# Banded attention with a gated MLP: K without one copy of the global keys, score blocks of 192, 224, 224 and 192 keys, and another order of weights in the values

## Chip, core and metric

The kernel runs on one NeuronCore of a Trainium2 chip. The metric is the device time of one execution in microseconds (us), the median of several runs. The engines are PE (TensorE, matrix products), DVE (VectorE), ACT (ScalarE) and POOL (GpSimd); SP issues the DMAs.

## What is computed

Eight batches with eight heads of 64 columns; 512 local tokens and 32 global ones. A global token attends to all 544 tokens. A local token attends to the 32 global tokens and to the local ones at a distance of at most 32. The result, token by token with all heads side by side, goes through a gated MLP: a product of two projections, then two more matrices.

```python
k_all = np.concatenate([k_g, k_l], axis=2)
v_all = np.concatenate([v_g, v_l], axis=2)
out_g = np.matmul(sm(scale * np.matmul(q_g, k_all.transpose(0, 1, 3, 2))), v_all)
mask = np.abs(pos[:, None] - pos[None, :]) <= window          # window = 32
s_ll = np.where(mask, scale * np.matmul(q_l, k_l.transpose(0, 1, 3, 2)), -1000000000.0)
s_lg = scale * np.matmul(q_l, k_g.transpose(0, 1, 3, 2))
out_l = np.matmul(sm(np.concatenate([s_lg, s_ll], axis=-1)), np.concatenate([v_g, v_l], axis=2))
...
h = (x @ w1) * (x @ w2) @ w3
return (h @ w_out).astype(np.float32)
```

## The kernel before

**Keys and scores.** A head's 512 local queries are four blocks of 128. A block needs its own 128 keys, 32 keys on either side (one side only at the ends) and the 32 global keys. The host lays K out so that each block's keys lie in one piece: k0, g, k1, g, k2, g, k3 (k0 to k3 are the local blocks, g the global keys), 608 columns. WIN (L22) gives each block's first column and width: (0, 192), (96, 256), (256, 256), (416, 192). The middle blocks read 256 columns, in which the global keys stand twice; the mask hides the second copy. `load_k2` (L372) fetches K of two heads, the 64 rows of either head one above the other in 128 partitions; `scores` (L479) makes all blocks of both heads, one head on the upper and one on the lower 64 rows of the array. Only the first two heads go through `scores1` (L466), one at a time. Each float32 product is executed as two instructions.

**Softmax.** `minus_max` (L494, DVE) reads a block's scores from PSUM, adds the mask from the constants `cs`, writes the block to the tile P and its minimum to `small`. `exps` (L503, ACT) takes exponentials in place and sums them. PAT (L23) says where each block lies in P.

**Turning the weights.** The values need the exponentials with the keys in the partitions. For the first eight heads PE transposes them (`transposes`), and ACT and DVE copy the pieces into the tiles PT (local keys) and G (global keys; `pieces`, `weights_hi`). From the ninth head on DVE transposes blocks of 32x32 (`turn` for the edges and the global columns, `turn_own` for the block's own keys); the latter go through DRAM (tile od) and come back turned as the tile own. There every number is split into a high and a low float32r part, both in PT and G.

**Values.** `values` (L615) makes the product with V for one head in two halves x. A half begins with a product with the global keys' V (L630), then come two key blocks j (L636). From the ninth head on each key block has two products: y = 0 is the high part of the weights with 128 columns of V (high and low part of V), y = 1 is the low part with V's 64 high columns. So V, the stationary operand, has 128, 64, 128, 64 columns in a row.

**MLP.** `first` (L787 to L789) and `second` (L819 to L821) run for 256 tokens at a time between the heads; at the start `fold` (L921) multiplies the last two matrices into one.

**Order.** PLAN (L70) lists all steps by number, with the engine that runs each; the list is the program's order, and every engine works its own steps through in that order. The numbers are those of the calls of `add`. All DMAs go out from SP in this order.

Of the kernel before, what the change touches and what calls it, by code (L numbers as in the profile page):

```python
# [20 lines left out]
KD = 608  # L21
WIN = [(0, 192), (96, 256), (256, 256), (416, 192)]  # L22
PAT = [0, 192, 448, 704]  # L23
PW = 896
# [6 lines left out]
def i(ap):  # L31
# [8 lines left out]
    qgl=(250, 461), vgh=606, vgl=(620, 1290), mmax=(437, 502), exps=(545, 592), inv=350, mul=(420, 740),  # L40
    hi=(587, 231, 231, 475, 294, 203, 256), hi_dve=(683, 260, 260, 540, 0, 0, 292), lo=(692, 253, 253, 559, 540, 247, 280), half=(470, 530), sum=520, join=485,
# [4 lines left out]
    scores1=1650, scores2=1910, ownt=780, ownl=(691, 1300), values32=(1180, 1130), gscores32=930, take=(446, 521), shiftp=(330, 300, 420),  # L46
# [24 lines left out]
    1V 790S 386S 3V 328S 791S 0S 390S 329S 8S 12S 16S 389S 5V 387P 792P 152S 846S 388D 793D 391P 795D 794A 797D 796A  # L71
    392D 798A 9D 393A 799D 10A 394D 800A 11D 395P 14A 13D 801P 20S 396A 397A 15D 802D 24S 18A 813P 845S 803D 804D 17D
    19D 805A 808A 806A 248P 807V 814D 816D 28S 809P 815A 399S 817A 158S 818D 820D 811P 819A 821A 22A 21D 825P 830A 23D
    826D 249P 32S 164S 827A 829A 828A 847P 822D 832A 810D 26A 823S 25D 27D 36S 900S 831V 812D 30A 258P 868D 848D 850D
    833P 835P 849A 852D 854D 853A 851A 29D 31D 398S 250P 863A 855A 862V 870D 40S 872D 400P 403S 874D 34A 33D 856P 834A
    875A 251P 166A 873A 836D 35D 44S 857A 259P 260P 837D 859D 869A 858D 7V 401D 899S 261P 861A 38A 860D 37D 864P 866P
    39D 871A 48S 876D 877S 42A 165D 167D 41D 865A 879P 43D 886A 885A 404P 52S 880D 884A 881A 330S 883A 262P 405D 882A
    46A 2V 887P 45D 406A 47D 252P 888A 56S 407D 824S 901P 953S 50A 49D 253P 902D 51D 867A 889P 54A 53D 60S 331A 55D
    903A 159D 254P 922D 924D 58A 64S 57D 255P 256A 59D 263P 264P 265P 890A 68S 257D 268P 269P 923A 891V 402S 154A 839V
    904D 906D 892V 270P 908D 408P 160A 842V 266A 267D 333A 62A 61D 878S 909A 925A 271P 63D 272P 332D 72S 65D 66A 843A  # L80
    67D 409A 273P 926D 76S 410A 928D 70A 278P 69D 71D 929A 274P 907A 844D 80S 917A 275P 153D 412S 893V 279P 276D 277D
    954S 280P 74A 73D 281P 905A 75D 84S 927A 282P 896D 78A 910P 77D 930D 931S 283P 284P 912D 911A 79D 933P 915A 914A
    155D 88S 82A 916V 81D 913A 285P 83D 92S 894A 413A 334D 918P 895D 286A 335S 414D 840A 920P 287D 841V 86A 932S 937A
    85D 87D 288P 289P 936A 838V 938A 934D 96S 290P 90A 89D 935A 291P 91D 919A 161D 955P 100S 94A 93D 336A 939A 95D 104S
    292P 921A 337V 940A 423S 976D 293P 956D 957A 978D 958D 941P 98A 960D 961A 294P 97D 99D 959A 415P 962D 110S 102A
    980D 295P 963A 943P 101D 982D 416A 103D 105D 106A 107D 964P 411S 942A 296A 965D 116S 298P 108V 944A 299P 968A 109D
    300P 301P 970A 424A 417D 945V 122S 112A 1008S 977A 111D 113D 983A 967D 946V 302P 303P 304P 297D 114A 115D 969A 966A
    971A 950D 305P 118A 128S 425D 1007S 979A 117D 951A 119D 981A 972P 974P 124A 984D 123D 985S 120A 125D 306A 121D 987P
    992A 426P 308P 309P 310P 947V 126A 993V 307D 134S 427A 990D 127D 130A 129D 991A 311P 140S 131D 312P 897A 428D 898V
    132A 313P 429A 133D 989D 988A 146S 430D 1082S 973A 952V 431D 975A 136A 314P 135D 432S 315P 316A 994A 137D 1155S  # L90
    948A 1009P 338S 141D 142A 949V 138V 139V 1040D 439S 1010D 1041A 1012D 1081S 1230S 1011A 1014D 318P 319P 986S 1013A
    1016D 148A 1042D 320P 1017A 1015A 321P 322P 433S 147D 149D 150A 143D 1043A 1024D 1028A 323P 324P 325P 151V 144A
    1044D 1046D 1025D 1026S 995P 997P 326A 317D 1029V 1032S 1047A 327D 418S 1045A 996D 145V 168A 1048D 1049S 1083P 156A
    6V 169D 182S 998A 157D 4V 162A 440A 999D 1001D 170S 3087P 3089P 1002A 163D 176S 1004D 1030A 1003D 3088P 3090P 1027S
    1031A 441D 1020A 1005A 1000V 419A 421A 3091P 1058D 1021V 420V 3095A 1057D 1114D 3093P 184A 422D 1229S 1061A 183D
    185D 1033S 172A 3092P 3094P 3101P 3102P 186A 171D 173D 178A 1059S 177D 1022A 187D 174A 179D 450S 1018A 175D 180A
    1084D 1085A 1086D 200S 1088D 1087A 188S 1116D 1115A 3096D 1089A 1062V 1065S 1019V 1023V 434S 1006V 3097A 1118D
# [187 lines left out]
def band_attention_glu_kernel(  # L285
# [20 lines left out]
    nc = tc.nc  # L306
# [6 lines left out]
    S = 544  # L313
# [13 lines left out]
    mask = cs[:, 128:384]  # L327
    masks = [cs[:, 384:576], mask, mask, mask[:, 0:192]]
# [13 lines left out]
    def constants():  # L342
        nc.sync.dma_start(cs, cst)

# [183 lines left out]
    def transposes(n):  # L528
        P = Ps[n % NP_]
        tt = T["tt", n] = ps_1.tile([128, 2, 4, 128], F32, tag="pu", name=f"t{n}", bufs=2)  # L530
        for e in range(4):
            nc.tensor.transpose(tt[:, 0, e, :], P[:, 256 * e : 256 * e + 128], ident)
        for e in range(3):
            nc.tensor.transpose(tt[:, 1, e, :], P[:, 256 * e + 128 : 256 * e + 256], ident)
# [50 lines left out]
    def pieces(n, e):  # L585
        plain = n < NF
        PT, G = M["PT", plain], M["G", plain]
        if e in (4, 5):
            TGr, TGg = T["TG", n // 4]
            c = 32 * (n % 4)  # L590
            if e == 4:
                r = TGr[:, n % 4].rearrange("p (a b q) -> p a b q", a=2, b=2)
                return r, gslots(PT, 0), gslots(PT, 1)
            return TGg[:, c : c + 32], G[0:32, 0:32], G[32:64, 0:32]
        if not plain:
            return T["own", n].rearrange("p (a x) -> p a x", a=4), *(PT[:, 2:6, y].rearrange("p a j q -> p a (j q)") for y in range(2))
        tt = T["tt", n]
        if e == 0:
# [16 lines left out]
    def values(n, x):  # L615
# [16 lines left out]
        for j, o, s0, s1 in ((2, 0, 0, 7), (3, 160, 1, 7)) if x else ((0, 0, 1, 7), (1, 128, 1, 8)):  # L632
            v = (T["vr", n // 2][:, j] if plain else T["vs", n // 2][:, n % 2, j]).rearrange("p a b -> p (a b)")
            for y in range(1 if plain else 2):
                r = 64 if y else 128
                nc.tensor.matmul(av[0:r, o : o + 32 * (s1 - s0)], v[:, 0:r], PT[:, s0:s1, y, j], start=False,  # L636
                                 stop=(j % 2 == 1 and (plain or y == 1)), skip_group_check=True)
# [395 lines left out]
    def head(n):  # L1033
# [354 lines left out]

    for key, users in late:
        after[key] += [u for u in users if u != key]  # L1390
# [73 lines left out]
```

## Time and profile before

| | |
|---|---|
| median of 3 runs | 809.75 us (809.15 to 809.78) |
| profiled execution | 809.29 us, of which its span 807.5 us |
| busy: PE, DVE, ACT, POOL | 794.4, 531.2, 455.3, 390.9 us |
| granted PE clock, mean | 0.995 |
| DMA | 128.85 MB in 191554 packets |

The span reaches from the first to the last instruction; the rest of the execution's time lies around it. Busy time is summed over stages that differ: the start (to 21 us), the first eight heads with the folding of matrices (to 105), the passage to the split numbers (to 150), the long stretch with heads and MLP together (to 702) and the MLP's rest. A chain of waits is followed back from the last instruction: each piece is what released the piece behind it.

### The profile page before, as it was taken

What the parts mean: (1) busy time and instruction counts of PE and PEld (TensorE: products, weight loads), DVE (VectorE), ACT (ScalarE), POOL (GpSimd) and SP (SyncE); (2) the same over time, 40 slices, a digit from 0 to 9 for tenths busy, and PEclk for the clock granted to TensorE, in tenths of its full rate; (3) what the DMA queues carried; (4) which work ended last, traced back from release to release, by engine and by line L of the source; (5) the groups of instructions that cost most, each with busy time, mean ns of one, the idle gap of its engine ahead of it and who ended that gap; (6) DMA issues with size and microseconds to landing.
All of it is one profiled execution on the core that took longest, in us unless ns stands there. A gap on an engine that the chain in (4) does not pass through costs nothing.

```text
span 807.5 us, 17227 instructions
## 1 busy us (share of the span) xinstructions
PE 794.4 (98%) x5608; PEld 704.6 (87%) x5608; DVE 531.2 (66%) x1504; ACT 455.3 (56%) x1290; POOL 390.9 (48%) x603
## 2 busy tenths in 40 slices
PE   9999989799999999999999999999999999999998
PEld 7656568699999999999999999999998999999997
DVE  4877978878777666677688867666576587612111
ACT  4767877776555545466665757665566554412011
POOL 1122354666555657656546556546556565412110
PEclk9999999999999999999999999999999999999999
DMA  8887877866557457565666656666664555300000
GB/s 275 266 267 226 262 193 193 207 171 187 160 151 206 122 155 180 144 188 138 162 174 170 202 157 169 177 171 173 187 171 130 137 152 153 97 27 14 15 27 26
DMA packets 191554, 128.85 MB, mean 160 GB/s; under 512 B 114472, under 2 KB 151592, under 8 KB 191464
## 3 DMA queue, kind: packets, MB, share of 16 engines
q1 hardware_dynamic: 191464, 127.75, 57.7%
q8 instruction: 44, 0.72, 0.4%
q14 instruction: 46, 0.38, 0.1%
HBM read 92.73 MB, written 34.96 MB: 158 GB/s over the span
## 4 chain that ended last, share of the span: by engine, by line
PE 94%; DVE 2%; ACT 1%; DMA 1%; SPq 1%; issue 0%; POOL 0%; ACTq 0%; DVEq 0%; POOLq 0%
PE bp L787 8%; PE ap L787 8%; PE acc L821 8%; PE acc L820 8%; PE acc L819 8%; PE bp L788 7%; PE bp L789 7%; PE ap L788 7%; PE ap L789 7%; PE w L921 7%; PE av L636 7%; PE s L491 6%; PE av L630 2%; PE sg L686 2%; DMA own<-od 1%; PE idle L364 1%
## 5 line engine op out<-in xcount | busy, mean ns | idle before, releaser
L787 PE MATMUL bp<-x,w12h 128*128 128x256 f32 x544 | 153.0, 281 | 0.0
L787 PE MATMUL ap<-x,w12h 128*128 128x256 f32 x544 | 152.5, 280 | 0.0
L788 PE MATMUL bp<-x,w12h 128*128 128x256 f32 x544 | 151.0, 278 | 0.0
L789 PE MATMUL bp<-x,w12l 128*128 128x256 f32 x544 | 150.8, 277 | 0.0
L788 PE MATMUL ap<-x,w12h 128*128 128x256 f32 x544 | 150.6, 277 | 0.0
L789 PE MATMUL ap<-x,w12l 128*128 128x256 f32 x544 | 150.5, 277 | 0.0
L504 ACT ACTIVATE P<-P,small 128x256 f32<-128x256 f32 (+1 forms) x256 | 121.6, 476 | 25.9 <-DVE small L500 25.1
L787 PEld LDWEIGHTS ap<-x,w12h 128*128 128x128 f32 x544 | 102.1, 188 | 4.0 <-issue 2.9
L787 PEld LDWEIGHTS bp<-x,w12h 128*128 128x128 f32 x544 | 102.6, 189 | 3.3 <-issue 2.2
L788 PEld LDWEIGHTS bp<-x,w12h 128*128 128x128 f32 x544 | 102.7, 189 | 0.7
L788 PEld LDWEIGHTS ap<-x,w12h 128*128 128x128 f32 x544 | 102.3, 188 | 0.7
L789 PEld LDWEIGHTS bp<-x,w12l 128*128 128x128 f32 x544 | 102.6, 189 | 0.0
L789 PEld LDWEIGHTS ap<-x,w12l 128*128 128x128 f32 x544 | 102.2, 188 | 0.0
L500 DVE CUSTOM_DVE_ANT_0 P<-s,cs 128x192 f32<-128x192 f32 (+1 forms) x256 | 86.1, 383 | 7.1 <-PE s L491 4.2
L650 DVE TENSOR_TENSOR u<-av,cb 64x352 f32<-64x352 f32 x112 | 55.7, 517 | 33.3 <-ACT cb L417 30.9
L417 ACT COPY cb<-av 64x352 f32<-64x352 f32 x71 | 30.6, 446 | 61.3 <-PE av L636 46.8
L636 PE MATMUL av<-PT,vs 128*128 128x192 f32 x448 | 62.0, 266 | 0.6 <-POOL PT L420 0.6
L921 PE MATMUL w<-wo,w3f 128*128 128x512 f32 x128 | 58.7, 597 | 0.3 <-DVE wo L845 0.3
L491 PEld LDWEIGHTS s<-kq,qp 64*128 64x128 f32 x496 | 43.3, 186 | 15.6 <-issue 6.5
L420 POOL TENSOR_TENSOR TT<-TT 128x352 fp32r<-128x352 f32 x38 | 38.5, 1013 | 35.7 <-ACT TT L417 20.5
L491 PE MATMUL s<-kq,qp 64*128 64x192 f32 (+1 forms) x496 | 55.4, 362 | 0.0
L636 PEld LDWEIGHTS av<-PT,vs 128*128 128x128 f32 x448 | 53.0, 164 | 2.7 <-POOL PT L420 0.8
(818 smaller groups left out, 1872.5 us busy)
## 6 DMA issues: line engine op xcount, KB each, us to landing
od<-tw SPq DMA_DIRECT2D x56, 256.0 KB, 2.6
own<-od SPq DMA_DIRECT2D x224, 64.0 KB, 2.4
raw_w<-in_w_t_dram SPq DMA_DIRECT2D x24, 512.0 KB, 4.9
kq<-in_kd_t_dram SPq DMA_DIRECT2D x32, 304.0 KB, 3.6
kpr<-in_kp_t_dram SPq DMA_DIRECT2D x32, 272.0 KB, 3.9
out_dram<-o_None SPq DMA_DIRECT2D x33, 256.0 KB, 2.8
qp<-in_q_t_dram SPq DMA_DIRECT2D x32, 256.0 KB, 3.7
R<-rd SPq DMA_DIRECT2D x64, 128.0 KB, 3.1
```

What stands on the lines that cost most here:

```text
L491: nc.tensor.matmul(st[:, x, c : c + w], q[r, 128 * e : 128 * e + 128], k[r, o : o + w], start=(e % 2 == 0), stop=True, skip_group_check=True)
L500: nc.vector.tensor_tensor_reduce(blk(n, e), s, masks[e], -0.125, 3.0e38, ALU.add, ALU.min, T["mn", n][:, e : e + 1])
L504: nc.scalar.activation(blk(n, e), blk(n, e), AF.Exp, bias=T["mn", n][:, e : e + 1], scale=-1.0, accum_out=T["sm", n // 2][:, n % 2, e : e ...
L636: nc.tensor.matmul(av[0:r, o : o + 32 * (s1 - s0)], v[:, 0:r], PT[:, s0:s1, y, j], start=False, stop=(j % 2 == 1 and (plain or y == 1)), s ...
L650: nc.vector.tensor_add(T["u", n // 2][r : r + 64, x], T.pop(("av", n, x))[r : r + 64, 0:352], T["cb", n][r : r + 64, x])
L787: nc.tensor.matmul(d, wh[:, k, c, :], x[:, 0, 0:w], start=(k == m % 2 == 0), stop=False, skip_group_check=True)
L788: nc.tensor.matmul(d, wh[:, k, c, :], x[:, 1, 0:w], start=False, stop=False, skip_group_check=True)
L789: nc.tensor.matmul(d, wl[:, k, c, :], x[:, 0, 0:w], start=False, stop=(k == 3), skip_group_check=True)
L819: nc.tensor.matmul(a, gh[:, m % 2, sl], wh[:, c], start=(m == 0), stop=False, **part)
L820: nc.tensor.matmul(a, gh[:, m % 2, sl], wl[:, c], start=False, stop=False, **part)
L821: nc.tensor.matmul(a, gl[:, m % 2, sl], wh[:, c], start=False, stop=(m in (5, 7)), **part)
L921: nc.tensor.matmul(T["w34", t], T["w3f", t, j // 4][:, j % 4], T["wo"][:, j], start=(j == 0), stop=(j == 7))
```

## The change

The layout in DRAM stays. `load_k2` fetches each row in two pieces, k0, g, k1 and k2, g, k3, and leaves out the copy of g between them: 576 columns. The blocks become 192, 224, 224 and 192 columns wide. The order inside the third block differs now from that inside the second (own keys before the global ones), so each of them has a mask of its own. The new step `order_masks` makes them from the loaded constants with two small copies on POOL; it stands early in PLAN as 3877V (V is POOL), between 0S, the load of the constants, and 5V, the clearing of G. Where P is read, the places follow. In the second key block of each half of the values, the product with 64 weight columns goes ahead of that with 128. Otherwise PLAN is the same. `COST` is not read by this list order.

```diff
-KD = 608
-WIN = [(0, 192), (96, 256), (256, 256), (416, 192)]
-PAT = [0, 192, 448, 704]
-PW = 896
+KD = 576
+WIN = [(0, 192), (96, 224), (256, 224), (384, 192)]
+PAT = [0, 192, 416, 640]
+PW = 832
...
-    mask = cs[:, 128:384]
-    masks = [cs[:, 384:576], mask, mask, mask[:, 0:192]]
+    masks = [cs[:, 384:576], cs[:, 128:352], cs[:, 352:576], cs[:, 128:320]]
...
+    def order_masks():
+
+        nc.gpsimd.tensor_copy(cs[:, 320:352], cs[:, 352:384])
+        nc.gpsimd.tensor_copy(cs[:, 352:384], cs[:, 128:160])
...
-        nc.sync.dma_start(kr, kd_t[b, 2 * p : 2 * p + 2].rearrange("h d s -> (h d) s"))
+
+        k = kd_t[b, 2 * p : 2 * p + 2].rearrange("h d s -> (h d) s")
+        nc.sync.dma_start(kr.rearrange("p (a s) -> p a s", a=2), view(k, 0, [320, 2], [1, 288]))
...
-        nc.vector.transpose(view(t, 32, [256, 3], [64, 3], [1, 32]), view(P, 160, [32, 3], [256, 3], [1, 32]))
-        nc.vector.transpose(t[:, 7, 1], P[:, 128:160])
+        nc.vector.transpose(view(t, 32, [256, 2], [64, 3], [1, 32]), view(P, 160, [32, 2], [224, 3], [1, 32]))
+        nc.vector.transpose(view(t, 480, [64, 2], [128, 2], [1, 32]), view(P, 128, [96, 2], [448, 2], [1, 32]))
...
-        nc.vector.transpose(view(t[:], 0, [32, 4], [128, 4], [1, 32]), view(P, 0, [256, 4], [32, 4], [1, 32]))
+        nc.vector.transpose(view(t[:], 0, [64, 2], [32, 2], [128, 4], [1, 32]), view(P, 0, [448, 2], [256, 2], [32, 4], [1, 32]))
...
-            3: (tt[96:128, 1, 0:3].rearrange("p a b -> p (a b)"), G[0:32, 160:S], None),
-            6: (tt[0:32, 1, 0], G[0:32, 32:160], None),
+            3: (tt[96:128, 1, 0:3:2], g_own[:, :, 1], None),
+            6: (tt[0:32, 1, 0:3:2], g_own[:, :, 0], None),
...
-            for y in range(1 if plain else 2):
+            ys = (0,) if plain else (1, 0) if j % 2 else (0, 1)
+            for y in ys:
                 r = 64 if y else 128
...
-                [("s", n) if n < 2 else ("sp", n // 2), *([("mmax", n, e - 1)] if e else [("load", "cs")])], minus_max, n, e)
+                [("s", n) if n < 2 else ("sp", n // 2), *([("mmax", n, e - 1)] if e else [("masks",)])], minus_max, n, e)
...
+    add(("masks",), only("POOL", 200, True), -30.0, [("load", "cs")], order_masks)
```

What stands in a row on PE for one pair of heads' scores (s from kq, the K of the pair, and qp, its Q), with the neighbours, before and then now. The last numbers of a row are the partitions or weight columns and the columns of the product:

```order
L921 MATMUL w_0_225<-wo,w3f_0_181 128x512
L491 MATMUL s_0_271<-kq_215,qp_152 128x192 x2
L491 MATMUL s_0_271<-kq_215,qp_152 128x256 x2
L491 MATMUL s_1_276<-kq_215,qp_152 128x256 x2
L491 MATMUL s_1_276<-kq_215,qp_152 128x192 x2
L921 MATMUL w_1_298<-wo,w3f_0_220 128x512
```

```order
L929 MATMUL w_0_227<-wo,w3f_0_183 128x512
L497 MATMUL s_0_273<-kq_217,qp_154 128x192 x2
L497 MATMUL s_0_273<-kq_217,qp_154 128x224 x2
L497 MATMUL s_1_278<-kq_217,qp_154 128x224 x2
L497 MATMUL s_1_278<-kq_217,qp_154 128x192 x2
L929 MATMUL w_1_300<-wo,w3f_0_222 128x512
```

The rows stay where they were; the four in the middle (two rows, two heads each) have 224 columns in place of 256.

On PE the values of one head (av from G, PT, and the global keys' V vgs and the pair's V vs), both halves, up to the first product of the MLP behind them, before and now:

```order
L630 MATMUL av_2444<-G_1039,vgs 128x288
L636 MATMUL av_2444<-PT_1046,vs_2274 128x192
L636 MATMUL av_2444<-PT_1046,vs_2274 64x192
L636 MATMUL av_2444<-PT_1046,vs_2274 128x224
L636 MATMUL av_2444<-PT_1046,vs_2274 64x224
L630 MATMUL av_2444<-G_1039,vgs 128x256
L636 MATMUL av_2444<-PT_1046,vs_2274 128x224
L636 MATMUL av_2444<-PT_1046,vs_2274 64x224
L636 MATMUL av_2444<-PT_1046,vs_2274 128x192
L636 MATMUL av_2444<-PT_1046,vs_2274 64x192
L787 MATMUL bp_0_0_2457<-x_0_0_1814,w12h_88 128x256
```

```order
L637 MATMUL av_2446<-G_1041,vgs 128x288
L644 MATMUL av_2446<-PT_1048,vs_2276 128x192
L644 MATMUL av_2446<-PT_1048,vs_2276 64x192
L644 MATMUL av_2446<-PT_1048,vs_2276 64x224
L644 MATMUL av_2446<-PT_1048,vs_2276 128x224
L637 MATMUL av_2446<-G_1041,vgs 128x256
L644 MATMUL av_2446<-PT_1048,vs_2276 128x224
L644 MATMUL av_2446<-PT_1048,vs_2276 64x224
L644 MATMUL av_2446<-PT_1048,vs_2276 64x192
L644 MATMUL av_2446<-PT_1048,vs_2276 128x192
L795 MATMUL bp_0_0_2459<-x_0_0_1816,w12h_88 128x256
```

In both halves the fourth and the fifth product have changed places: the 128-wide one comes last.

On POOL, where the next head's weights are written into PT (TGr holds the turned weights of the global queries; CAST writes the high part, the TENSOR_TENSOR behind it the low part), with the semaphores that each instruction waits for, before and now:

```order
L420 TENSOR_TENSOR PT_1046<-TGr_1713,PT_1046 128x2x2x32 [waits Activation_49]
L526 TENSOR_TENSOR u_1585<-u_1585,R_1612 128x256 [waits DMAHW5_49,DMAHW4_49]
L417 CAST kph_1948<-kpr_1822 128x544 [waits DMAHW2_49,PE_49]
L417 CAST PT_1046<-TGr_1713 128x2x2x32 [waits PE_49,Pool_49]
L420 TENSOR_TENSOR PT_1046<-TGr_1713,PT_1046 128x2x2x32 [waits PE_49,Pool_49]
```

```order
L426 TENSOR_TENSOR PT_1048<-TGr_1715,PT_1048 128x2x2x32 [waits Activation_49]
L532 TENSOR_TENSOR u_1587<-u_1587,R_1614 128x256 [waits DMAHW5_49,DMAHW4_49]
L423 CAST kph_1950<-kpr_1824 128x544 [waits DMAHW2_49,PE_49]
L423 CAST PT_1048<-TGr_1715 128x2x2x32 [waits PE_49,Pool_49]
L426 TENSOR_TENSOR PT_1048<-TGr_1715,PT_1048 128x2x2x32 [waits Pool_49]
```

The instructions stand as before; the low part's writer no longer waits for PE, since the high part's writer ahead of it now waits for the later product.

## Rows read from the trace of the kernel before

**Rows 1.** The page's chain that ended last, share of the span by engine.

```profile
PE 94%; DVE 2%; ACT 1%; DMA 1%; SPq 1%; issue 0%; POOL 0%; ACTq 0%; DVEq 0%; POOLq 0%
```

**Rows 2.** Stretches: length, then PE, PEld, DVE, ACT, POOL busy, clock, DMA share, GB/s.

```profile
21.00:105.00 84.00, 83.93 (x325) 49.51 (x326) 69.20 (x191) 62.23 (x168) 20.55 (x31) 1.00 0.82 253
...
150.00:702.00 552.00, 551.77 (x4181) 510.49 (x4182) 397.36 (x1145) 329.64 (x959) 325.19 (x509) 1.00 0.62 165
```

**Rows 3.** Waits, whole run: us in total, times, longest; PE's two longest and POOL's.

```profile
PE av L630 <- DVE small L717: 3.8, 1, 3.8
PE av L630 <- ACT P L504: 2.8, 1, 2.8
...
POOL PT L417 <- PE av L636: 65.1, 24, 7.0
```

**Rows 4.** Scores: group of the page; PE's timeline (start, us) in short windows; chain.

```profile
L491 PE MATMUL s<-kq,qp 64*128 64x192 f32 (+1 forms) x496 | 55.4, 362 | 0.0
...
280.84 0.55 PE L491 MATMUL s<-kq,qp 64*128 64x192 f32 x4
...
281.00 0.60 PE L491 MATMUL s<-kq,qp 64*128 64x256 f32 x4
...
281.22 0.60 PE L491 MATMUL s<-kq,qp 64*128 64x256 f32 x4
...
280.64 1.72 PE s L491 x16
282.36 0.31 PE bp L787
```

**Rows 5.** The chain in order of time (start, us, what), first head's scores.

```profile
7.46 1.71 PE s L476 x8
```

**Rows 6.** Groups by shape on DVE, the masked minimum: busy us, mean ns | idle before.

```profile
L500 DVE CUSTOM_DVE_ANT_0 P<-s,cs 128x256 f32<-128x256 f32 x128 | 49.7, 416 | 0.2
L500 DVE CUSTOM_DVE_ANT_0 P<-s,cs 128x192 f32<-128x192 f32 x128 | 43.3, 350 | 6.8 <-PE s L491 4.2 <-PE s L476 1.4
```

**Rows 7.** Values: weight loads by shape (PEld), then the chain around one head's values.

```profile
L636 PEld LDWEIGHTS av<-PT,vs 128*128 128x128 f32 x224 | 42.6, 190 | 1.9
L636 PEld LDWEIGHTS av<-PT,vs 128*64 128x64 f32 x224 | 30.7, 137 | 0.8 <-POOL PT L420 0.8
...
294.66 0.23 PE acc L821
294.89 0.13 PE av L630
295.02 0.41 PE av L636 x4
295.43 0.12 PE av L630
295.55 0.39 PE av L636 x4
295.95 0.14 PE bp L787
...
296.44 0.11 PE bp L788
```

**Rows 8.** DMA issues of the page: count, KB each, median us from issue to landing.

```profile
od<-tw SPq DMA_DIRECT2D x56, 256.0 KB, 2.6
...
kq<-in_kd_t_dram SPq DMA_DIRECT2D x32, 304.0 KB, 3.6
```

**Rows 9.** The chain in order of time, its two longest pieces between 105 and 150 us.

```profile
112.78 5.26 DMA own<-od
...
143.41 4.66 DMA own<-od
```

**Rows 10.** DVE's timeline at the start: start, us, instruction, idle before and releaser.

```profile
7.03 0.72 DVE L705 CUSTOM_DVE_ANT_1 Pg<-sg,cs 64x544 f32<-64x544 f32 x1 [5.90 <-DMA cs<-in_cst_dram]
...
9.49 0.42 DVE L500 CUSTOM_DVE_ANT_0 P<-s,cs 128x256 f32<-128x256 f32 x1
```

More of the change, by code (lines that the diff above doesn't have):

```diff
@@ L39 @@
     kh=703, kl=(790, 1500), qh=617, ql=(620, 1290), vh=404, vl=(545, 746), kph=647, kpl=(726, 1374), qgh=298,
-    qgl=(250, 461), vgh=606, vgl=(620, 1290), mmax=(437, 502), exps=(545, 592), inv=350, mul=(420, 740),
-    hi=(587, 231, 231, 475, 294, 203, 256), hi_dve=(683, 260, 260, 540, 0, 0, 292), lo=(692, 253, 253, 559, 540, 247, 280), half=(470, 530), sum=520, join=485,
+    qgl=(250, 461), vgh=606, vgl=(620, 1290), mmax=(437, 470), exps=(545, 568), inv=350, mul=(420, 740),
+    hi=(587, 231, 231, 366, 294, 203, 366), hi_dve=(683, 260, 260, 416, 0, 0, 416), lo=(692, 253, 253, 559, 540, 247, 280), half=(470, 530), sum=520, join=485,
     joing=750, xh=405, xl=(411, 740), cg=610, mg=790, eg=840, ng=820, wg=(683, 292), ga=588, gb=691, gh=620,
@@ L45 @@
     gtrans=465, own=355, turn=650, gturn=1010, edge=(513, 520), edgel=(520, 960), first=1372, second=1382, fold=860,
-    scores1=1650, scores2=1910, ownt=780, ownl=(691, 1300), values32=(1180, 1130), gscores32=930, take=(446, 521), shiftp=(330, 300, 420),
+    scores1=1543, scores2=1610, ownt=780, ownl=(691, 1300), values32=(1180, 1130), gscores32=930, take=(446, 521), shiftp=(330, 300, 420),
 )
@@ L76 @@
[L76 to L80, printed above, removed]
@@ new lines @@
+    23D 826D 249P 32S 164S 827A 829A 828A 847P 822D 832A 810D 26A 823S 25D 27D 36S 900S 831V 812D 30A 258P 868D 848D
+    850D 833P 835P 849A 852D 854D 853A 851A 29D 31D 398S 250P 863A 855A 862V 870D 40S 872D 400P 403S 874D 34A 33D 856P
+    834A 875A 251P 166A 873A 836D 35D 44S 857A 259P 260P 837D 859D 869A 858D 7V 401D 899S 261P 861A 38A 860D 37D 864P
+    866P 39D 871A 48S 876D 877S 42A 165D 167D 41D 865A 879P 43D 886A 885A 404P 52S 880D 884A 881A 330S 883A 262P 405D
+    882A 46A 2V 887P 45D 406A 47D 252P 888A 56S 407D 824S 901P 953S 50A 49D 253P 902D 51D 867A 889P 54A 53D 60S 331A
@@ new lines @@
+    55D 903A 159D 254P 922D 924D 58A 64S 57D 255P 256A 59D 263P 264P 265P 890A 68S 257D 268P 269P 923A 891V 402S 154A
+    839V 904D 906D 892V 270P 908D 408P 160A 842V 266A 267D 333A 62A 61D 878S 909A 925A 271P 63D 272P 332D 72S 65D 66A
+    843A 67D 409A 273P 926D 76S 410A 928D 70A 278P 69D 71D 929A 274P 907A 844D 80S 917A 275P 153D 412S 893V 279P 276D
+    277D 954S 280P 74A 73D 281P 905A 75D 84S 927A 282P 896D 78A 910P 77D 930D 931S 283P 284P 912D 911A 79D 933P 915A
+    914A 155D 88S 82A 916V 81D 913A 285P 83D 92S 894A 413A 334D 918P 895D 286A 335S 414D 840A 920P 287D 841V 86A 932S
@@ new lines @@
+    937A 85D 87D 288P 289P 936A 838V 938A 934D 96S 290P 90A 89D 935A 291P 91D 919A 161D 955P 100S 94A 93D 336A 939A 95D
+    104S 292P 921A 337V 940A 423S 976D 293P 956D 957A 978D 958D 941P 98A 960D 961A 294P 97D 99D 959A 415P 962D 110S
+    102A 980D 295P 963A 943P 101D 982D 416A 103D 105D 106A 107D 964P 411S 942A 296A 965D 116S 298P 108V 944A 299P 968A
+    109D 300P 301P 970A 424A 417D 945V 122S 112A 1008S 977A 111D 113D 983A 967D 946V 302P 303P 304P 297D 114A 115D 969A
+    966A 971A 950D 305P 118A 128S 425D 1007S 979A 117D 951A 119D 981A 972P 974P 124A 984D 123D 985S 120A 125D 306A 121D
@@ new lines @@
+    987P 992A 426P 308P 309P 310P 947V 126A 993V 307D 134S 427A 990D 127D 130A 129D 991A 311P 140S 131D 312P 897A 428D
+    898V 132A 313P 429A 133D 989D 988A 146S 430D 1082S 973A 952V 431D 975A 136A 314P 135D 432S 315P 316A 994A 137D
+    1155S 948A 1009P 338S 141D 142A 949V 138V 139V 1040D 439S 1010D 1041A 1012D 1081S 1230S 1011A 1014D 318P 319P 986S
+    1013A 1016D 148A 1042D 320P 1017A 1015A 321P 322P 433S 147D 149D 150A 143D 1043A 1024D 1028A 323P 324P 325P 151V
+    144A 1044D 1046D 1025D 1026S 995P 997P 326A 317D 1029V 1032S 1047A 327D 418S 1045A 996D 145V 168A 1048D 1049S 1083P
@@ L530, in transposes @@
         tt = T["tt", n] = ps_1.tile([128, 2, 4, 128], F32, tag="pu", name=f"t{n}", bufs=2)
[L531 to L534, printed above, removed]
+        for e, c in enumerate((0, 256, 448, 704)):
+            nc.tensor.transpose(tt[:, 0, e, :], P[:, c : c + 128], ident)
+        for e, c in enumerate((128, 352, 576)):
+            nc.tensor.transpose(tt[:, 1, e, :], P[:, c : c + 128], ident)
     def turn(n):
         P, t = Ps[n % NP_][:], f(TT[:])
-        nc.vector.transpose(view(t, 32, [256, 3], [64, 3], [1, 32]), view(P, 160, [32, 3], [256, 3], [1, 32]))
-        nc.vector.transpose(t[:, 7, 1], P[:, 128:160])
+        nc.vector.transpose(view(t, 32, [256, 2], [64, 3], [1, 32]), view(P, 160, [32, 2], [224, 3], [1, 32]))
+        nc.vector.transpose(view(t, 480, [64, 2], [128, 2], [1, 32]), view(P, 128, [96, 2], [448, 2], [1, 32]))
     def turn_own(n):
@@ L597, in pieces @@
         tt = T["tt", n]
+        g_own = G[0:32, 32:S].rearrange("g (c d x) -> g c d x", c=2, d=2)
         if e == 0:
```

31 lines of the change are left out of this document (8 added, 23 removed).

## Prediction

> **What bounds the kernel now.** I read the chain that ended last first: 94% of it is TensorE (PE), while DVE, ACT and DMA have 4% together [rows 1]. Then the stretches: from 150 to 702 us, two thirds of the span, PE is busy 551.77 of 552.00 us, and from 21 to 105 us 83.93 of 84.00; DVE, the next engine, is busy 72% of the long stretch [rows 2]. The list of waits says the same from the other side: PE's two longest waits are 3.8 and 2.8 us, once each, both in the passage between 105 and 151 us, and the longest total of all is POOL's, which waits for PE's values [rows 3]. So a nanosecond taken from PE's instruction stream shortens the span, one taken from DVE or ACT does not, and what the change adds elsewhere has to be large to be seen.
>
> **Scores: the term that carries the sum.** Each head has four key blocks; the two middle ones go from 256 to 224 columns. The number of instructions stays. Two heads run side by side on 64 rows each, and every product is two instructions: sixteen for a pair of heads, and 496 / 16 = 31 pairs [rows 4]. How long one takes is read from the distance between couples, one instruction of each head: the couple after one of 192 columns begins 281.00 - 280.84 = 0.16 us later, the couple after one of 256 columns 281.22 - 281.00 = 0.22 us later [rows 4]. That is 0.84 ns for a column (0.16 / 192 = 0.83, 0.22 / 256 = 0.86), so 32 columns are 27 ns. A pair of heads has four couples of 256 columns (two blocks, two instructions each) and loses 4 x 27 = 108 ns of its 1.72 us [rows 4]. The other bound: if the whole 1.72 us, entry and exit included, went by columns, 256 of 3584 would be 0.123 us. I take 0.108, since the distances are the nearer row. 31 x 0.108 = **3.35 us** (at most 3.8). Four of the pairs lie between 22 and 97 us and 27 after 155 us, all in stretches where PE is full [rows 2].
>
> **The first two heads** run alone, eight instructions in 1.71 us [rows 5], and lose 4 x 27 = 0.107 us each. The first stands in the chain of the start, with filler products behind it; the second does not, DVE reaches it late. Bounds 0 and 0.21, I take **0.1 us**, the one that the chain holds.
>
> **Softmax.** The masked minimum on DVE costs 416 ns at 256 and 350 at 192 columns [rows 6], so 33 ns less at 224, 128 times: 4.2 us of DVE; ACT's exponentials shrink likewise. In the long stretch both have idle time, so this counts nothing. Between 105 and 150 us, where both are busiest, it could give some tenths.
>
> **The weights turned over in the values.** Per head and half, PE runs one global product (288 or 256 columns) and four of 192 or 224 columns, with 128, 64, 128, 64 weight columns; now 128, 64, 64, 128. The load of the next weights runs beside the product before it. A load of 128 columns shows 190 ns, one of 64 shows 137 [rows 7]: 53 ns for 64 columns, so about 106 and 53 ns of loading proper. A product streams 512 columns in 0.23 us [rows 7], 0.45 ns a column: 256 columns take 115 ns, 224 about 100, 192 about 86. A 64-wide load always hides; a 128-wide one hides behind 256 or more, is 6 ns late behind 224 and 20 late behind 192. Before, the 128-wide loads stand behind 288, 192 and 224 columns (the last is that of the second half's global product), then behind 256, 224 and 192 (that of the next stage): late 20 + 6 + 6 + 20 = 52 ns. Now they stand behind 288, 224, 224, then 256, 192, 192: 6 + 6 + 20 + 20 = 52 ns. The first half gains 14 ns, the second loses 14. The rows of before fit: the four products of the first half take 0.41 us, those of the second 0.39, both 832 columns or 0.37 us of stream, and the next stage's first product shows 0.14 where 256 columns are 0.115 [rows 7]. So I take **0**; if the effect in only one half were real, it is 56 heads x 14 ns = 0.8 us to either side.
>
> **A wait that moves with it.** The next head's weights are written into PT when the last product that reads their part has gone. The high part is now read by the last product, not by the one before it: its writers on POOL and ACT (POOL's waits on PE's values alone are 24, [rows 3]) start one product later, about 0.1 us (0.39 / 4, [rows 7]), with all that is queued behind them on POOL and ACT; the low part's writer on POOL loses its wait on PE. From 151 us on this is covered, since PE then waits for none of them; with the cover gone it is 0.1 us a head. Between 105 and 150 us there are four heads: 0 to 0.4 us lost, and the narrower softmax may give as much back. Together 0, within 0.4 either way.
>
> **The rest.** K comes in two pieces per row, 2304 bytes in place of 2432 (304 KB in all, [rows 8]). The write of the turned scores, 256 KB in four pieces a row, lands in 2.6 us, the one-piece K load in 3.6 [rows 8]: smaller pieces show no price, and no wait of PE's after 151 us is on K. In the passage the chain hangs on the transfer own<-od, 5.26 and 4.66 us [rows 9]; the one K load near them is issued behind the first. 0, inside the 0.4 above. The two mask copies on POOL wait for the constants, which are there when DVE begins at 7.03; the first minimum that needs a copied mask begins at 9.49 [rows 10], so they have 2.4 us for 32 columns each. Nothing; were they as late as 10.5, the start would lose 1 us. The clearing of G, queued behind them, is needed only after the first head's transposes. The copies to G (384 and 128 columns become 256 and 256) and DVE's transposes (288 and 32 become 192 and 128) keep their sum and their number of instructions: nothing.
>
> **Sum.** 3.35 + 0.1 + 0 + 0 = 3.45 us. The profiled execution took 809.29 us (span 807.5 and 1.8 around it): 805.8. The median of the runs, 809.75, is 0.46 higher: 806.3. I say **806.0**, between them. Its own range: from 805.8 down by 0.46 (scores at their upper bound), 0.8 (values) and 0.4 (passage) to 804.1; from 806.3 up by 0.8, 0.4 and the 0.1 of the start to 807.6.
>
> **Rivals.** *A, the turn-over gains.* Each head changes eight times between 128 and 64 weight columns, now four times. What a head's values take over their stream is 1.05 us less 2208 columns x 0.45 ns, 0.06 us, and 0.03 at the next stage's product [rows 7]. If that were the price of the changes and not of late loads, half of 0.09 x 56 would go, 2.5 us: 803.5. Against it: the excess is as large as the late loads alone explain. The Trainium skill, "TensorEngine Tiling (Array Packing)", section Tiling Modes, Key Properties, says that a change of the tiling mode drains the engine, and lists 128x64 as a mode of its own; by that rule this rival would hold. The trace agrees for the scores on 64 rows, behind which the next product shows 0.31 us [rows 4]; for the width of the values it shows no such gap. Chance 0.09.
> *B, part of the gain stays behind.* PE gets ahead of its suppliers: the later writers of PT, or DVE, become the bound in some of the heads. For it: the moved wait, DVE at 72%. Against it: PE has no wait after 151 us, and its faster scores feed the same suppliers sooner. Half of 27 x 0.108 = 2.9 us lost: 807.5. Chance 0.13.
> *C, slower.* In the second half two 128-wide loads now follow each other behind 192 columns. After one late load the next stage's first four products take 296.44 - 295.95 = 0.49 us in place of 0.45 [rows 7], a debt of 0.04. If the debt grows with each late load in a row, the second adds its own 0.02 and up to twice 0.04: 0.10 us x 56 = 5.6, and 806.3 + 5.6 = 811.9. It turns the sign from 3.45 / 56 = 62 ns a head. Against it: the first half has one such load less, which should pay it back. Chance 0.04.
> That the change does not do what it says is excluded by the order of instructions: the scores stand there with 224 columns.
>
> **How the numbers follow.** Forecast 0.70, A 0.09, B 0.13, C 0.04, something that no row points to 0.04. The range reaches past B and a little towards A: 804.0 to 808.0. Measured differences under 0.2% (1.6 us) cannot be told from no change. The forecast, A and more than half of B lie below 808.1, the upper part of B and half of C within 0.2%: faster 0.86, same 0.10, slower 0.04.
>
> **What would show it.** Right: the sixteen score instructions of a pair in 1.61 us; the two halves of the values near 0.40 each, their sum unchanged; PE full from 151 us on; the passage as long as before. A would show both halves shorter; B new waits of PE on PT, G or vs after 151 us; C a second half above 0.45 us and a next stage's first product above 0.14. The prediction is wrong if the couple after one of 224 columns does not come 0.19 us later, or if the passage changes by more than 1 us.

## The result, and the profile after

| | before | after |
|---|---|---|
| median | 809.45 us (4 runs, 807.72 to 809.78) | 819.21 us (4 runs, 817.76 to 820.95) |
| profiled execution, its span | 809.29, 807.5 us | 818.64, 816.9 us |
| granted PE clock, mean | 0.995 | 0.997 |

The changed kernel is slower by 1.3%, little but clear of the scatter: ratio 1.0126, 95% interval 1.0100 to 1.0152, where 806.0 us was forecast. The page of after, busy times and the chain's shares:

```profile
span 816.9 us, 17175 instructions
...
PE 804.6 (98%) x5608; PEld 715.2 (88%) x5608; DVE 528.0 (65%) x1504; ACT 453.4 (55%) x1290; POOL 391.9 (48%) x605
...
PE 93%; DVE 2%; DMA 1%; ACT 1%; SPq 1%; issue 0%; POOL 0%; DVEq 0%; ACTq 0%; POOLq 0%
```

The bound is the same as in [rows 1]: PE's stream of instructions. It has grown by itself. The stretches of after (length, then PE, PEld, DVE, ACT, POOL busy, clock, DMA share, GB/s), and the last one of before, which was not shown:

```profile
150.00:702.00 552.00, 552.00 (x4128) 512.23 (x4127) 389.39 (x1134) 324.50 (x948) 321.74 (x501) 1.00 0.61 162
702.00:816.90 114.90, 111.11 (x787) 103.80 (x785) 21.15 (x34) 20.61 (x41) 18.95 (x26) 0.99 0.08 25
```

```profile
702.00:807.50 105.50, 101.75 (x741) 95.38 (x739) 17.38 (x27) 17.77 (x34) 16.16 (x20) 1.00 0.06 21
```

In the same 552 us PE is as full as in [rows 2], at the same clock, but gets through 4128 products in place of 4181. So products take longer, and no wait has come in: PE's two longest waits are 3.1 and 2.7 us, once each, where [rows 3] has 3.8 and 2.8 (the longer one is now put down to POOL, before to DVE). POOL's wait on the values has grown (65.1 to 74.9 us), but from 152 to 702 us neither trace shows a wait of PE for another engine.

```profile
PE av L637 <- POOL w12h L423: 3.1, 1, 3.1
PE av L637 <- ACT P L510: 2.7, 1, 2.7
...
POOL PT L423 <- PE av L644: 74.9, 25, 6.9
```

What the forecast of the scores rested on came: a pair of heads' scores takes 1.61 us in place of 1.72 [rows 4], and the masked minimum on DVE 382 ns at 224 columns [rows 6]. The chain of after, and DVE's group:

```profile
310.94 1.61 PE s L497 x16
312.55 0.31 PE ap L795
```

```profile
L506 DVE CUSTOM_DVE_ANT_0 P<-s,cs 128x224 f32<-128x224 f32 x128 | 45.5, 382 | 0.2
```

**Where the time came from.** The products of the MLP's first step (ap, bp: 256 columns, the lines L787 to L789 before, L795 to L797 after) start at another pitch. PE's timeline of before, then of after, at the first such products of the kernel; the columns are start and duration in us, and the second row of either kernel is 24 products after the first:

```profile
109.48 0.28 PE L788 MATMUL ap<-x,w12h 128*128 128x256 f32 x1
...
112.20 0.28 PE L788 MATMUL bp<-x,w12h 128*128 128x256 f32 x1
```

```profile
109.71 0.28 PE L796 MATMUL ap<-x,w12h 128*128 128x256 f32 x1
...
112.54 0.28 PE L796 MATMUL bp<-x,w12h 128*128 128x256 f32 x1
```

Before, 2.72 us / 24 = 113 ns; after, 2.83 / 24 = 118 ns. The durations say 0.28 in both: they overlap, and only the distance between starts shows it. The last 4,880 products of either trace are the same list but for the width of the scores and the order in the values. The distances behind the 3,094 of this kind among them add up to 356.5 us before and 367.7 after: 11.2 us more. The 512-column products (acc) take 1.75 more there, the values 0.3 more, and the scores give back 2.6: 10.7 us in all. After begins that stretch 1.4 us earlier (see Start and passage below), and so the spans differ by 9.4.

At 109 us no weight has been turned over yet: the first such head comes in the passage after it. So the turn-over can't be what makes these first products slow. What has also changed by then is where things lie. P shrinks from 896 to 832 columns and the K tiles from 608 to 576; whatever the program places behind them moves down. By the allocation, x goes from byte 97,600 of each partition to 97,088 (512 lower, two P tiles of 64 columns less) and w12, the MLP's first weights, from 162,944 to 162,048 (896 lower, with three K tiles of 32 columns less).

### The profile page after: what moved, and what is told of

Read it like the earlier page. It is cut to its first block, busy times and chain, and to the rows that moved or that the text cites. A ratio compares the mean times of both kernels' runs of the same rounds, so it can differ in the third digit from the quotient of the medians.

```text
span 816.9 us, 17175 instructions
## 1 busy us (share of the span) xinstructions
PE 804.6 (98%) x5608; PEld 715.2 (88%) x5608; DVE 528.0 (65%) x1504; ACT 453.4 (55%) x1290; POOL 391.9 (48%) x605
## 4 chain that ended last, share of the span: by engine, by line
PE 93%; DVE 2%; DMA 1%; ACT 1%; SPq 1%; issue 0%; POOL 0%; DVEq 0%; ACTq 0%; POOLq 0%
PE bp L795 8%; PE ap L795 8%; PE bp L797 8%; PE acc L827 8%; PE bp L796 8%; PE acc L829 8%; PE acc L828 8%; PE ap L797 8%; PE ap L796 8%; PE w L929 7%; PE av L644 7%; PE s L497 6%; PE av L637 3%; PE sg L694 2%; DMA raw_w<-in_w_t_dram 1%; DMA own<-od 1%
## 5 line engine op out<-in xcount | busy, mean ns | idle before, releaser
L795 PE MATMUL ap<-x,w12h 128*128 128x256 f32 x544 | 153.9, 283 | 0.0
L795 PE MATMUL bp<-x,w12h 128*128 128x256 f32 x544 | 153.9, 283 | 0.0
L797 PE MATMUL bp<-x,w12l 128*128 128x256 f32 x544 | 152.0, 279 | 0.0
L797 PE MATMUL ap<-x,w12l 128*128 128x256 f32 x544 | 152.0, 279 | 0.0
L510 ACT ACTIVATE P<-P,small 128x224 f32<-128x224 f32 (+1 forms) x256 | 118.8, 465 | 26.9 <-DVE small L506 25.9
L795 PEld LDWEIGHTS ap<-x,w12h 128*128 128x128 f32 x544 | 102.0, 188 | 4.0 <-issue 2.9
L795 PEld LDWEIGHTS bp<-x,w12h 128*128 128x128 f32 x544 | 102.1, 188 | 3.3 <-issue 2.7
L797 PEld LDWEIGHTS ap<-x,w12l 128*128 128x128 f32 x544 | 102.1, 188 | 0.0
L797 PEld LDWEIGHTS bp<-x,w12l 128*128 128x128 f32 x544 | 102.1, 188 | 0.0
L506 DVE CUSTOM_DVE_ANT_0 P<-s,cs 128x192 f32<-128x192 f32 (+1 forms) x256 | 81.8, 366 | 8.0 <-PE s L497 4.8
L644 PEld LDWEIGHTS av<-PT,vs 128*128 128x128 f32 x448 | 57.1, 162 | 2.8 <-POOL PT L426 0.9
L497 PE MATMUL s<-kq,qp 64*128 64x192 f32 (+1 forms) x496 | 52.1, 349 | 0.0
```

The lines of the kernel that those rows point to most:

```text
L497: nc.tensor.matmul(st[:, x, c : c + w], q[r, 128 * e : 128 * e + 128], k[r, o : o + w], start=(e % 2 == 0), stop=True, skip_group_check=True)
L506: nc.vector.tensor_tensor_reduce(blk(n, e), s, masks[e], -0.125, 3.0e38, ALU.add, ALU.min, T["mn", n][:, e : e + 1])
L510: nc.scalar.activation(blk(n, e), blk(n, e), AF.Exp, bias=T["mn", n][:, e : e + 1], scale=-1.0, accum_out=T["sm", n // 2][:, n % 2, e : e ...
L795: nc.tensor.matmul(d, wh[:, k, c, :], x[:, 0, 0:w], start=(k == m % 2 == 0), stop=False, skip_group_check=True)
L797: nc.tensor.matmul(d, wl[:, k, c, :], x[:, 0, 0:w], start=False, stop=(k == 3), skip_group_check=True)
```

## Experiments

**Places or order (e1 to e4).** The first theory: the MLP's products are slow because w12 and x lie elsewhere. Its rival: rival C of the prediction, with a debt that is never paid back.

e1, the changed kernel with the old order of weights:

```diff
-            ys = (0,) if plain else (1, 0) if j % 2 else (0, 1)
+            ys = (0,) if plain else (0, 1)
```

> The changed kernel with the old order of weights in the values (128, 64, 128, 64 columns); tiles stay where the change put them. Places theory: P and the K tiles became smaller, so the MLP's x and weight tiles lie 512 to 896 bytes lower in SBUF, and this alone makes each 256-column product of the MLP take 118 ns in place of 113. It expects the pitch 118 from the first such products at 109 us on and a time of 819 us, within 1. Order theory (rival C, a debt that is never paid back): pitch 113, and 806 us.

Measured 818.41 us (ratio to before 1.0113, 1.0087 to 1.0139), mean pitch after 155 us 118.9 ns as in after. Places.

e2, the changed kernel with the old places:

```diff
-    Ps = [const.tile([128, PW], F32, tag=f"P{e}", name=f"P{e}") for e in range(NP_)]
+    Ps = [const.tile([128, 896], F32, tag=f"P{e}", name=f"P{e}") for e in range(NP_)]
...
-        kr = p2.tile([128, KD], F32, tag="kr", name=f"kq{m}", bufs=NK)
+        kr = p2.tile([128, 608], F32, tag="kr", name=f"kq{m}", bufs=NK)[:, 0:KD]
...
```

> The changed kernel with the turned-over weights, but P tiles of 896 columns and K tiles of 608 columns of which only 832 and 576 are used, so that every tile lies where it lay before the change. Places theory: pitch 113, time 806 us, within 1 (the forecast). Order theory: pitch 118 and 819 us.

Measured 813.48 us (1.0034, 1.0019 to 1.0048): between the two, and so a miss for either theory alone. The MLP's first products are soon back at 113 ns, but behind most heads' values a stage runs at 118.

e3, the kernel before with the turn-over alone (in `values`):

```diff
-            for y in range(1 if plain else 2):
+            ys = (0,) if plain else (1, 0) if j % 2 else (0, 1)
+            for y in ys:
...
```

> The kernel before with the weights of the second key block turned over and nothing else. Places theory with the prediction's own term: 809.5 us, within 0.8, pitch 113. Rival A: 807 us. Order theory or rival C: 815 to 823 us, the pitch after a head's values above 113 for the whole stage.

Measured 816.45 us (1.0076, 1.0057 to 1.0095). Here the places theory missed: the turn-over costs time too.

e4, the kernel before with one unused tile (in `open_early`):

```diff
+        p2.tile([128, 32], F32, tag="pad", name="pad", bufs=1)
```

> The kernel before with an unused tile of 128 bytes per partition ahead of the K tiles: the K tiles and all behind them, the MLP's weights w12 among them, lie 128 bytes higher; x, PT and vs stay. Counted modulo 512 bytes, w12 then begins where the change put it (256, before 128). Places theory, if the place of w12 within 512 bytes decides: pitch 118 in the 256-column products, the 512-column ones as before, 820 us or a little more. If another tile or a longer distance decides, or order: 809.5 us.

Measured 822.44 us (1.0153, 1.0129 to 1.0176): 128 unused bytes cost 12 us, with every instruction and its order as before.

**The pitch measured by itself (e5).** Between two heads' values, 48 products go out as in the MLP, with w12 and x displaced:

```python
wh, wl = (at(W0 + w + 8192 * m + 4096 * e, 1024)... for e in range(2))
xh, xl = (at(X0 + x + 2048 * k + 1024 * e, 256) for e in range(2))
nc.tensor.matmul(d, wh[:, k, c], xh, ...)
nc.tensor.matmul(d, wh[:, k, c], xl, ...)
nc.tensor.matmul(d, wl[:, k, c], xh, ...)
```

> Only products on zeros, nothing of the reference is computed: on TensorE, without any other engine at work, one head's values (old order, then turned over), then 48 products of 256 columns as in the MLP, for 23 placings of the weights w12 and of x against their places in the kernel before (in steps of 64 bytes), and 18 placings for the MLP's products of 512 columns. Places theory: behind the old order 113 ns at the old places, 118 at the places of after (w12 896 bytes lower, x 512) and of e4 (w12 128 higher), and a rule in bytes between; behind the turned order 118 at the old places too, as in e2 and e3. Rival: other engines' reads and writes of SBUF, or the transfers, make the slower pitch; then 113 (or one value) at all places here.

Two of the 46 stretches, at the old places and with w12 256 bytes further (the second row of each is 24 products after the first):

```profile
45.06 0.28 PE L74 MATMUL ab<-big 128*128 128x256 f32 x1
...
47.89 0.28 PE L74 MATMUL ab<-big 128*128 128x256 f32 x1
...
99.76 0.28 PE L76 MATMUL ab<-big 128*128 128x256 f32 x1
...
102.48 0.28 PE L76 MATMUL ab<-big 128*128 128x256 f32 x1
```

2.83 / 24 = 118 and 2.72 / 24 = 113 ns, with no other engine at work and no transfer: the rival falls. One expectation missed: at the old places the products take 118 behind the old order too, where the kernel before runs at 113. All placings, by how far the distance from x to w12 differs from that of before, modulo 256 bytes (mean of the last 25 distances between starts):

| distance against before | 256-column product | placings (w12, x moved by) |
|---|---|---|
| 0 | 113.3 to 113.4, or 117.8 at two of nine | 117.8: 0/0, 256/256; 113.3: 256/0, 512/0, 1024/0, 0/256, 0/-512, 128/128, 384/384 |
| 64 | 118.6 to 118.7 | 64/0, 320/0, 0/192, 0/448 |
| 128 | 117.8 | 128/0, 384/0, 0/128, 0/384, -896/-512 (after) |
| 192 | 120.0 | 192/0, 448/0, 0/64, 0/320 |

The rule is the distance of the two operands: moving either by the same amount the other way gives the same pitch, in the steps of 64 bytes tried here. After's -896 + 512 = -384 is 128 modulo 256, like e4's. The 512-column products (g the weights, w34 the moving operand) go by distance too: 226.6 ns where g stands 64 bytes further against w34, about 229 at the old distance, 231 to 235 at the others. What the table leaves open is the first row: at distance 0 there are two pitches.

**Putting it together (e6, e7).** e6 has e2's places and e1's order; e7 is e2 with the turn-over in the first half alone:

```diff
-            ys = (0,) if plain else (1, 0) if j % 2 else (0, 1)
+            ys = (0,) if plain else (1, 0) if j == 1 else (0, 1)
```

> The changed kernel's narrower K and score blocks alone, with the old order of weights in the values and every tile at its old place (P of 896 and K tiles of 608 columns, partly unused). If the turn-over and the moved places are the two whole causes, what is left is the prediction's own sum without them: 810.2 - 3.4 = 806.8 us, within 0.8, pitch 113 to the end. If a third cause is in the K part: above 808.5.

> As e6, and the weights turned over in the first half of each head's values alone, so that the last product before the MLP has 64 weight columns again. If it is the 128-wide load behind the last 192 columns that sends the MLP's products into the slower pitch: 113 to the end and 806.0 us (14 ns a head less than e6), within 0.8. If the turn-over does it in either half: 813 us and pitch 118 in part of the stages.

Measured: e6 806.10 us (0.9952, 0.9934 to 0.9969), e7 805.16 us (0.9948, 0.9928 to 0.9968), mean pitch 115.3 ns in both, as before. Both beat both kernels. PE in e6 in the long stretch:

```profile
150.00:702.00 552.00, 552.00 (x4199) 512.89 (x4200) 394.73 (x1146) 328.52 (x962) 325.30 (x509) 1.00 0.61 164
```

4199 products, where before had 4181 [rows 2] and after 4128. With e1, e2 and after, the four corners stand:

| | old order of weights | turned over |
|---|---|---|
| tiles at their old places | 806.1 (e6) | 813.5 (e2) |
| tiles as the change puts them | 818.4 (e1) | 819.2 (after) |

The places cost 12.3 us; the turn-over 7.4 at the old places and 0.8, within the scatter of the runs, at the new ones. They don't add up because they slow the same products: over the last 4,880, e2 takes 7.1 us more than e6, 5.8 of them in the MLP's first step, which after's places slow already.

**Values, and the rule in the whole kernel (e8 to e10).** e8 displaces V and the global keys' V, and w12 and w34 in finer steps.

> Products on zeros alone again, nothing of the reference is computed: (1) 256-column MLP products at the old places behind either order of the values, with and without 512-column products ahead of the values, and with either half of w12 first, (2) w12 moved by 4 to 224 bytes, (3) values with V 0 to 192 bytes and the global keys' V 0 to 192 bytes further, (4) 512-column products with w34 160 to 224 bytes further. Places theory (what counts is the distance of the weights from the moving operand, modulo 256 bytes): (1) 113 or 118, the one or the other by the way in; (2) 117 to 120 at all, if the steps are as coarse as 64 bytes then 4 to 48 as at 0; (3) blocks of values of different length, by up to 3 ns a product; (4) 226.6 at 192, 229 to 234 at others. Rival: distance plays no part outside the two kinds of products seen so far; then the blocks in (3) are of one length.

Measured: (1) 118 in all eight; (2) 117.3 to 120.0 at every step from 4 to 224 bytes (with 118 at the old places themselves here, so how many bytes the good distance bears stays open); (3) blocks of values that follow one another between 1.07 and 1.10 us at all 16 placings, without order: the rival holds for the values. But where V lies does reach the stage of the MLP behind them, with w12 and x left where they are: 13 of the 32 such stages take 118, the others 113; (4) 226.6 at 192, 232 to 237 at 160, 176, 208 and 224.

e9 is the changed kernel with a larger unused tile in `open_early`:

```diff
+        p2.tile([128, 224], F32, tag="pad", name="pad", bufs=1)
```

> The changed kernel as it is, turn-over included, with an unused tile of 896 bytes per partition behind the K, Q and output tiles, so that w12 lies where it lay before the change and x 512 bytes lower: a distance of a multiple of 256 bytes again. In e5 this placing took 113 ns behind either order. Places theory: 805.5 us, within 1, if the way in is as in e5; 813 us if the turn-over sends half of the stages to 118 as in e2. If the distance is not what counts in the whole kernel: 819 us.

Measured 813.72 us (1.0055, 1.0033 to 1.0076): an unused tile takes back 5.5 us. The rest is the turn-over's, as in e2 (as many stages stay slow, see the table below): the way in was not as in e5.

e10 is e9 with e7's line and two unused tiles more, behind xg:

```diff
+    const.tile([128, 48], F32, tag="pad34", name="pad34")
+    p1.tile([128, 16], F32, tag="pad1", name="pad1")
```

> A version that may beat both: the changed kernel with the dead tile of e9, the weights turned over in the first half of the values alone as in e7, and w34, the weights of the MLP's second product, 192 bytes further against gh and gl (which with all other tiles keep their distances modulo 256). In e5 the 512-column products took 226.6 ns there, against 229 on the mean at the old distance. Places theory: 816 x 2.5 = 2.0 us less than e7's 805.2, so 803.2, within 1. Rival: the second product does not go by distance in the whole kernel: 805.2.

Measured 810.22 us (1.0010, 0.9994 to 1.0025), a miss. Some 512-column products run at 226 to 228 ns, others at 231 to 236, and the stages of the MLP's first step directly behind them now take 118 (all 28 of twelve products or more after 160 us; in e7 none): mean 116.3 against e7's 115.3, 3.1 us over 3096 products, of 5.1 between the two kernels. A stage that is faster by itself can hand on a worse way in.

**Which half, and another place (e11, e12).** e11 is e2 with the turn-over in the second half alone; e12 has after's tiles with e7's order and a pad of 128 bytes:

```diff
-            ys = (0,) if plain else (1, 0) if j % 2 else (0, 1)
+            ys = (0,) if plain else (1, 0) if j == 3 else (0, 1)
```

```diff
-            ys = (0,) if plain else (1, 0) if j % 2 else (0, 1)
+            ys = (0,) if plain else (1, 0) if j == 1 else (0, 1)
...
+        p2.tile([128, 32], F32, tag="pad", name="pad", bufs=1)
```

> As e6 (narrower K and blocks, every tile at its old place), the weights turned over in the second half of each head's values alone. If the way into the MLP's products decides between 113 and 118 ns at the old distance, this half alone costs what both cost in e2: 813.5 us, within 1, and after most heads' values 118 for the whole first stage. If both halves share the cost: 809 to 810 us.

> The smaller tiles of the changed kernel, the turn-over in the first half alone (as e7), and an unused tile of 128 bytes ahead of w12, so that w12 stands 768 bytes lower than before, x 512: neither is where it was, their distance has changed by 256 bytes. Distance rule: 113 to the end, or nearly, and 805.2 us, within 1; up to 813 if the way in is poor at this place. If w12's own place decides (it lies where no run had it): 818.5 us as in e1.

Measured: e12 806.35 us (0.9960, 0.9945 to 0.9975), with w12 where no other run had it: distance, not place. e11 806.41 us (0.9968, 0.9950 to 0.9985), a surprise, where 813.5 was expected: the late loads in a row cost little by themselves (18 ns a head, see below). How many stages stay slow, of the 45 of at least twelve products that follow a head's values directly after 160 us (mean of the 9th to 12th distance above 116 ns):

| before | e6 | e7 | e11 | e12 | e3 | e2 | e9 | after, e1, e4 |
|---|---|---|---|---|---|---|---|---|
| 0 | 0 | 3 | 6 | 3 | 42 | 42 | 42 | 45 |

The chain of e2, then of e11, at the same head (start, us, what); the last row is twelve products after the one before it:

```profile
295.48 0.41 PE av L644 x4
295.88 0.14 PE bp L795
...
296.97 0.12 PE bp L795
...
298.38 0.12 PE bp L795
```

```profile
294.86 0.41 PE av L644 x4
295.27 0.14 PE bp L795
...
296.33 0.11 PE bp L795
...
297.69 0.11 PE bp L795
```

Both second halves take 0.41 us with the 128-wide product last, both stages begin with 0.14; one goes on at 1.41 / 12 = 118, the other at 1.36 / 12 = 113.

**The way in (e13).** A head's values, one product of n columns, then 24 as in the MLP:

```python
nc.tensor.matmul(av[0][:, 0:n], at(W0 + w, 128), at(X0, n), ...)   # n = 64, 72, ... 256
```

> Products on zeros alone, nothing of the reference is computed: one head's values (either order), one product of 64 to 256 columns in steps of 8, then 24 products of 256 columns as in the MLP, with w12 at its old place and 512 bytes further (both a distance of 0 modulo 256 to x as before). Two-pitch theory: at one and the same place both pitches occur, 113 behind some widths of the product in between and 118 behind others, each staying to the end of the stage; then the turn-over in e2 and e3 costs time because it changes the way in, not because 128-wide loads stand in a row. Rival: one pitch at each place whatever comes ahead (118 at the old place, 113 at 512 bytes further, as in e5); then what the turn-over did in e2 and e3 needs another cause.

PE's timeline behind n = 160 and n = 168, nothing else changed, old places, old order (the third row of each is 18 products after the second):

```profile
90.03 0.26 PE L89 MATMUL av<-big 128*128 128x160 f32 x1
...
90.75 0.28 PE L71 MATMUL ab<-big 128*128 128x256 f32 x1
...
92.87 0.28 PE L71 MATMUL ab<-big 128*128 128x256 f32 x1
...
94.05 0.27 PE L89 MATMUL av<-big 128*128 128x168 f32 x1
...
94.76 0.28 PE L71 MATMUL ab<-big 128*128 128x256 f32 x1
...
96.80 0.28 PE L71 MATMUL ab<-big 128*128 128x256 f32 x1
```

2.12 / 18 = 118 and 2.04 / 18 = 113 ns. Of the 25 widths, 10 give 118 behind the old order and 6 behind the turned one, the same ones at both placings, and the pitch stays to the end of the stage. The two-pitch theory holds and the rival falls: at one distance both pitches last to the end of a stage, and what PE does just before chooses. By what rule it chooses, no run shows.

## Why the prediction was wrong, point by point

**What bounds the kernel: right.** PE's stream set the end in every run.

**Scores: right.** 1.61 us a pair, forecast 1.61; the first head's eight products take 1.60 in e6, forecast 1.71 - 0.11. What the K part is worth without the rest is e6: 810.15 - 806.10 = 4.0 us (2.5 to 5.3 by its interval), forecast 3.45; e6's runs also had the higher granted clock, 0.996 on the mean against 0.994. Over the last 4,880 products the scores' distances are 2.56 us less in e6 than before, 107 ns for each of the 24 pairs there, forecast 108. One reading was off: two of the 27 pairs said to lie after 155 us lie in the passage (at 107.5 and 135.9 us), where PE also stands and waits; that is 0.2 us of the term.

```profile
7.69 1.60 PE s L482 x8
```

**The rest, "nothing": the step that failed first.** It priced the narrower K and P by what they read, write and wait for. That a smaller tile moves all tiles behind it stood nowhere in the sum, and that is 12.3 us (e1 against e6) of the 13.2 by which the forecast was short, 128 bytes alone being enough (e4). No row of before could have priced it; the diff's `PW` and `KD` could have raised the question. For the transfers, mask copies and copies to G, e6 leaves no cost that could be seen; they were not tested one by one.

**The values, "So I take 0": the second.** The term itself is about right in size: counted between starts, a head's values, 1,057 ns before, take 1,065 turned over (e2: +8; 56 heads are 0.5 us), 1,049 with the first half alone (e7: -8, forecast -14) and 1,075 with the second alone (e11: +18, forecast +14). What failed is the price of the next stage: the late load before it was to leave a debt of 0.04 us, and of the first half, with one such load less, the prediction says that it "should pay it back". The rows of before show the stage's first four products at 0.49 us [rows 7] and were read as a debt that ends; it ends only if the stage falls into the 113. In e2 it doesn't, 42 times of 45, against none in e6: 7.4 us. The chain of after, at the head of [rows 7], where the places alone would hold the pitch at 118 as well:

```profile
295.40 0.23 PE acc L829
295.63 0.13 PE av L637
295.77 0.40 PE av L644 x4
296.16 0.13 PE av L637
296.29 0.41 PE av L644 x4
296.70 0.14 PE bp L795
296.84 0.12 PE bp L796
...
297.78 0.12 PE bp L795
```

**Rival C** had the right sign and, at 5.6 us, nearly the price of the turn-over at the old places (7.4), but another mechanism, so that the numbers lie close by luck: two late loads in a row in the second half are what e11 has, for 18 ns a head in place of 100, and either half turned over alone leaves most stages at 113 (e7, e11), while both together do not (e2).

**Rival A** falls. With half the changes between 128 and 64 weight columns a head's values take 8 ns more, not 45 less. The Trainium skill's rule that it was compared with ("TensorEngine Tiling (Array Packing)", Tiling Modes, Key Properties: a change of mode drains the engine) has no gap here to stand for.

**Rival B** falls: PE waits for none of its suppliers in the long stretch of after or of e6, though in after POOL waits 10 us more for PE.

**Start and passage: the granted clock.** After reaches the product that before starts at 150.2 us 1.3 us earlier, though it starts the first scores of the global queries 0.6 later; e6 starts those 0.2 later (5.64 against 5.41 us) and is 0.3 earlier at that product. The stretch from 121 to 124 us of before, then of after (columns as in [rows 2]):

```profile
121.00:124.00 3.00, 3.00 (x17) 3.00 (x16) 1.42 (x3) 1.84 (x6) 1.68 (x5) 0.50 1.07 299
```

```profile
121.00:124.00 3.00, 3.00 (x26) 3.00 (x27) 2.35 (x8) 2.54 (x9) 2.74 (x6) 1.00 1.03 309
```

Before ran it at a granted clock of 0.50, the level of 1.2 GHz, after at 1.00, that of 2.4: 17 products against 26. In the 4 us ahead, from 116 to 120, PE had been busy for 1.69 us in before and 2.24 in after. The 501st to 600th product of the program, which span this, take 17.4 us in before and 16.3 in after. E6 (0.54 in this stretch) and e10 are like before in it, e1, e2 and e7 like after, so single executions don't show that the change decides which comes. What starts those first scores later in after and e6 stays open (e10 starts them at 5.24). The prediction's own mark, a passage that changes by more than 1 us, was crossed in after, but in after's favour; it isn't where the 9.8 us are.

## What to carry to other kernels

Before a tile is made smaller, see what lies behind it, and try the change once with the old places held by padding: only that tells the edit from the move. Where PE is full, read the distance between starts of equal products in equal stages, since busy shares, waits and durations can all stay the same while the stream slows down. An order of products that costs nothing by itself can still hand the next stage another pitch.

## What the runs showed of the hardware that was not expected

The pitch of 256-column float32r products with 128 weight columns goes by the distance in bytes between weights and moving operand, modulo 256: at best 113.3 ns at the distance of before (65,344 bytes, 64 modulo 256), 117.8 to 120.0 at distances 64, 128 and 192 further (e5). At the good distance two pitches exist, 113.3 and 117.8; each lasts to the end of a stage of 24 to 48 products, and which one a stage gets depends on the products just ahead, down to 8 columns in the width of one (e13). That holds with no other engine running.

The Trainium skill, "TensorE: Matmul & The Clock Gate", section Step-by-step: what each phase is for, says that weights and moving operand come through two independent read ports, so that loading the next weights takes no read bandwidth from the running product. By that alone the distance between the two should not matter; in the runs it does: with the same instructions, 128 bytes between the two make 4.5 ns a product (e4, e5). What couples the two inside the chip no run here shows; that the reads meet is one reading, and it was not tested apart.
